# Second-layer sums in PSUM, one scratch pool, first w1 operands made earlier

## The chip, the core and the metric

One core of one Trainium2 chip. The metric is the device time of one execution in microseconds (us), median of several runs. TensorE is PE, VectorE DVE, ScalarE ACT, GpSimd POOL; SP is the queue that issues all transfers.

## What is computed

Linear attention on 4 batches of 8 heads (576 tokens, 64 wide), then two layers on the 2304 tokens of width 512:

```python
# attention, per head; phi(x) = [exp(p), exp(-p)], p = x@w_phi - max|x@w_phi|
kv = k_p^T v;  z = sum(k_p);  x = (q_p kv) / (q_p z + 1e-6)
# first layer, 512 -> 2048 -> 512
h = x @ w_in;  x = max(0.01*h, h) @ w_out
# second layer: 4 experts of 512 -> 1024 -> 512, mixed by normalised domain_probs
for e in range(4): out += p[:, e:e+1] * (max(x @ w1[e], 0) @ w2[e])
```

## The kernel before

All large products are made in three matmuls of float32r operands: a value is split into a high half (`hi`, a copy that rounds) and a low half (`lo`, the difference), and hi*hi, hi*lo and lo*hi are summed in PSUM (`PASS`).

The program is one plan: a list of (time, function) sorted by time (line 816), so the text order of attention steps (`TIMES`, line 39, stretched by `LO` and `HI`) and of first-layer steps (`moe1_group`, line 557) is set by numbers. Attention of batch b+1 runs beside the first layer of batch b. The instructions are then ordered per engine by the tile framework, which may run a later one first when an earlier one still waits. A pool is a ring of equal buffers; a tile waits until one is free.

Attention works pair of heads by pair: loads `kraw` and `qraw`, key features (`kp`, `kt`), `kv`, query features (`pc`, `mb`, `e`, split into `qh` and `ql`), numerators (`nf`), the division by way of DRAM (`ds`, `dr`, `rb`), and the result `xr`, split into `xh` and `xl`. Its scratch tiles of 2304 bytes come from `ap_` (`N_A` = 17 buffers, line 104), opened on the right side of SBUF; the first layer's `hs` and `g` come from `up` (`N_U` = 4, line 98). Line 107 chooses. In the first layer each of 64 blocks F (16 per batch) has an up product (`moe1_up`, tile `hp`), the leaky relu (`hs`, `g`, split into `gt`) and, in groups of four blocks, down products (`moe1_down`, tile `op`), summed into `acc`, one per batch. The last group, after the loops, holds only down products (line 814).

The second layer uses Strassen-like products: tokens in 3 blocks j of two halves of 384, and for each of 16 pairs c of w1 column blocks seven products of half-size operands (`PRODUCTS`, line 652), 48 steps k = 16 j + c. Operands of the tokens (`x2_steps`, line 602: b11, t1, b21, t2, b22, t3, t4, each split) are cut from `acc`; their raw differences lie in `xt`; the halves lie three to a buffer, five buffers to a block, from the list `kind` (`xp` or `x2p`). The difference and the low half are made on POOL, the high half on ACT. Operands of w1: `w2_raw` (line 660) loads two raw blocks into `r`, makes four sums on POOL, and `w2_split` (line 677) makes `wuh` on ACT and `wul` on POOL; w2 is split in `w2_split_d`. All of these pools are opened at line 819, when the first layer's pools are closed, over the same addresses; a tile waits only for the old tiles that it covers.

A step runs `up_a` (products 1, 5, 2, 6, 3, 7), the split of the next step's w1, `down(k-1, 1)`, `up_b` (product 4), `down(k-1, 0)`. In `up_a` product 1 goes to px, is copied to py (the start of product 6's sum), product 2 is added in px; product 5 goes to pv, is copied to ss, product 3 is added in pv. The sums pv + ss and py + ss go to SBUF (`c`), and `relu` makes the high half gh on ACT and the low half gl on VectorE. `down` multiplies gh and gl by w2, and VectorE adds p times the result to `ob`.

Of the kernel before, what the change touches and what calls it, by code (L numbers as in the profile page):

```python
# [16 lines left out]
DF = 128  # L17
# [51 lines left out]
N_U = 4  # L69
N_A = 17  # L70
# [10 lines left out]
def body(ctx, tc, kT, qT, vh, w_phi, w_in, w_out, probs, w1, w2, out):  # L81
# [14 lines left out]
    left, right = ExitStack(), ExitStack()  # L96
    RIGHT = "right"
    up = opened(left, "up", N_U)
    wp = opened(left, "wp", N_W)
    wrp = opened(left, "wrp", 4)  # L100
# [3 lines left out]
    ap_ = opened(right, "ap", N_A, side=RIGHT)  # L104
    vp = opened(right, "vp", 2, side=RIGHT)

    def unit(name, dt=F32):
        pool = up if name in ("hs", "g") else ap_
        return pool.tile([128, S], dt, tag="u", name=name)
# [76 lines left out]
    def k_feat(b, hp, g):  # L186
        if g == 0:
            kfs[b, hp] += (
                xp.tile([128, 2, 4, 2, DF], F32, tag="x", name="kp"),
                ap_.tile([128, 2, 2, DF], F32, tag="u", name="kt"),  # L190
            )
# [24 lines left out]
        nc.vector.tensor_reduce(  # L216
            out=m[0:r, 0:nb], in_=pv, op=ALU.max, axis=AX.X, apply_absolute_value=True
        )
        if INPL[b] or nb == 8:
            y = pv  # L220
        else:
            y = ap_.tile([128, 4, DF], F32, tag="u", name="ky")[0:r, 0:nb]
# [15 lines left out]
    def kv_side(b, hp, h):  # L238
# [18 lines left out]
        if h == 1:  # L257
            if "n" in DIRECT[b]:
                kv = ap_.tile([128, 4, 128], F32, tag="u", name="kv")
# [3 lines left out]
            kvh = ap_.tile([128, 4, 128], F32R, tag="u", name="kvh")  # L263
            kvl = ap_.tile([128, 4, 128], F32R, tag="u", name="kvl")
# [395 lines left out]
    def w2_raw(c):  # L660

        r = m2["r"].tile([128, 8, 256], F32, tag="r", name="r")
        nc.sync.dma_start(out=r[:, 2:4].rearrange("p a f -> p (a f)"), in_=w1[2 * c])
        nc.sync.dma_start(out=r[:, 0:2].rearrange("p a f -> p (a f)"), in_=w1[2 * c + 1])
        r2 = m2["r2"].tile([128, 2, DM], F32, tag="r2", name="r2")
        for t in range(2):
            nc.sync.dma_start(out=r2[:, t], in_=w2[2 * c + t])
        for o, x, y, op in (
            (4, 0, 1, ALU.add),
            (5, 4, 2, ALU.subtract),  # L670
            (6, 2, 0, ALU.subtract),
            (7, 3, 5, ALU.subtract),
        ):
            nc.gpsimd.tensor_tensor(out=r[:, o], in0=r[:, x], in1=r[:, y], op=op)  # L674
        return r, r2
# [143 lines left out]
    for name, bufs in (("r", 1), ("r2", 1), ("wu", 4), ("wd", 2), ("h", 4), ("sum", 2), ("ob", 1)):  # L819
        m2[name] = opened(left, "m2" + name, bufs)  # L820
    for name, bufs in (("px", 2), ("py", 1), ("pv", 1), ("po", 4)):
        m2[name] = opened(left, name, bufs, space=bass.MemoryType.PSUM)
    m2["y"] = m2["py"].tile([128, 512], F32, tag="y", name="py")[:, 0:TH]
    n = NB * NC2
    raw = w2_raw(0)
    w2_split(0, raw)
    w2_split_d(0, raw)
    nxt = []
    for k in range(n):
# [12 lines left out]
        if raw:  # L842
            w2_split_d(k + 1, raw)
# [5 lines left out]
    right.close()  # L849
# [33 lines left out]
```

## Time and profile before

| | |
|---|---|
| Median of 3 runs (lowest, highest) | 1439.45 us (1437.5, 1463.09) |
| Profiled execution: own time, span | 1447.1 us, 1445.3 us |
| PE busy | 1399.8 us, 97% of the span |
| DVE, ACT, POOL busy | 884.1, 657.6, 605.0 us |
| Mean granted clock of PE, whole span | 0.982 |
| Attention alone, then beside the first layer | 0 to about 100, to about 540 us |
| First layer alone | to 677 us |
| Second layer | to the end |

Matmuls are pipelined, so a busy PE need not be at its peak; idle time of another engine costs nothing by itself. In a timeline row the bracket gives the idle time of the engine before it and what ended it. The views are of the profiled execution.

### The profile page before, as it was taken

The page shows a single profiled execution, that of the slowest core. Times are in us where ns is not written, and L with a number is a line of the kernel's source. Part 1 is how long each engine was busy: PE and PEld are TensorE (multiplying, and loading weights), DVE is VectorE, ACT ScalarE, POOL GpSimd, SP SyncE. Part 2 cuts the span into 40 slices and gives each one's busy share as a digit, 9 for nine tenths or more (in the row PEclk, how much of TensorE's full clock was granted, in tenths as well). Part 3 has the DMA queues.
Part 4 walks back from the last instruction along what each step waited for, and adds up shares of the span by engine and source line. Part 5 has one row for each costly group of instructions (what it writes and reads, how often), then busy time and mean ns, then how long its engine had stood idle before and what let it go on. Part 6 is the DMA issues. An engine that isn't in the chain of part 4 may idle for free.

```text
span 1445.3 us, 20868 instructions
## 1 busy us (share of the span) xinstructions
PE 1399.8 (97%) x8105; PEld 1282.1 (89%) x8105; DVE 884.1 (61%) x1270; ACT 657.6 (45%) x1201; POOL 605.0 (42%) x413
## 2 busy tenths in 40 slices
PE   8969998999999989999999999999999999999998
PEld 5758988999899989999789899989989999999997
DVE  4459888757676655653546556555566455655655
ACT  4537665656565733533433433353433333333432
POOL 2222101111111122402966656687665665665651
PEclk9969999999999999999999999999999999999999
DMA  5346474323333222321212221221212123222121
GB/s 191 90 133 220 175 257 132 108 76 114 92 108 94 70 68 66 95 83 47 74 56 75 71 73 59 73 102 60 87 59 73 59 81 110 59 73 73 59 73 44
DMA packets 77266, 134.11 MB, mean 93 GB/s; under 512 B 12016, under 2 KB 21360, under 8 KB 77168
## 3 DMA queue, kind: packets, MB, share of 16 engines
q1 hardware_dynamic: 77168, 132.79, 28.8%
q8 instruction: 63, 1.03, 0.3%
q14 instruction: 35, 0.29, 0.1%
HBM read 119.51 MB, written 13.18 MB: 92 GB/s over the span
## 4 chain that ended last, share of the span: by engine, by line
PE 82%; DMA 7%; DVE 5%; POOL 3%; issue 2%; ACT 1%; SPq 0%; DVEq 0%; POOLq 0%; ACTq 0%
PE po L770 26%; PE op L542 12%; PE hp L510 11%; PE py L699 10%; PE px L699 6%; PE pv L699 6%; PE kvp L250 5%; DMA rb<-dr 3%; PE nm L342 2%; PE pk L211 2%; DMA w<-w 1%; DMA qraw<-qT 1%; POOL wul L683 1%; DMA r<-w 1%; PE pq L296 1%
## 5 line engine op out<-in xcount | busy, mean ns | idle before, releaser
L770 PE MATMUL po<-wd,gh 128*128 128x512 f32 x1152 | 387.9, 392 | 0.2 <-ACT gh L713 0.2
L784 DVE SCALAR_TENSOR_TENSOR ob<-po,pe,ob 128x512 f32<-128x512 f32 x270 | 193.5, 747 | 174.7 <-PE po L770 174.1
L770 PEld LDWEIGHTS po<-wd,gh 128*128 128x128 f32 x1152 | 214.7, 188 | 32.9 <-ACT gh L713 0.5
L683 POOL TENSOR_TENSOR wul<-r,wuh 128x1024 fp32r<-128x1024 f32 x96 | 203.2, 2134 | 93.5 <-ACT wuh L682 93.5
L303 POOL PARTITION_ALL_REDUCE mb<-pc x32 | 72.3, 2261 | 403.6 <-ACT pc L301 319.1
L674 POOL TENSOR_TENSOR r<-r 128x256 f32<-128x256 f32 x192 | 148.0, 792 | 216.5 <-DMA r<-w 213.5
L542 PE MATMUL op<-gt,wt 128*128 128x288 f32 x1536 | 224.8, 300 | 12.0 <-DVE gt L122 9.1
L542 PEld LDWEIGHTS op<-gt,wt 128*128 128x128 f32 x1536 | 211.8, 191 | 16.0 <-DVE gt L122 10.0
L770 PE MATMUL po<-wd,gl 128*128 128x512 f32 x576 | 225.4, 391 | 0.5 <-DVE gl L714 0.5
L510 PE MATMUL hp<-xh,wt 128*128 128x288 f32 x1024 | 217.6, 298 | 4.5 <-ACT xh L121 4.2
L510 PEld LDWEIGHTS hp<-xh,wt 128*128 128x128 f32 x1024 | 168.6, 189 | 6.4 <-ACT xh L121 4.5
L714 DVE SCALAR_TENSOR_TENSOR gl<-s,gh 128x384 fp32r<-128x384 f32 x96 | 137.8, 1437 | 32.4 <-ACT gh L713 32.4
L682 ACT CAST wuh<-r 128x1024 fp32r<-128x1024 f32 x96 | 86.7, 941 | 149.6 <-issue 89.8
L510 PE MATMUL hp<-xl,wt 128*128 128x288 f32 x512 | 152.8, 299 | 0.4 <-DVE xl L122 0.4
L699 PE MATMUL py<-xo,wuh 128*128 128x384 f32 x576 | 149.3, 340 | 0.6 <-ACT s L741 0.6
L770 PEld LDWEIGHTS po<-wd,gl 128*128 128x128 f32 x576 | 108.2, 188 | 18.9 <-DVE gl L714 0.8
L690 POOL TENSOR_TENSOR wd<-r,wd 128x1024 fp32r<-128x1024 f32 x48 | 116.6, 2429 | 6.9 <-ACT wd L689 6.9
L699 PEld LDWEIGHTS py<-xo,wuh 128*128 128x128 f32 x576 | 106.1, 189 | 8.4 <-ACT s L741 1.1
L699 PE MATMUL px<-xo,wuh 128*128 128x384 f32 x384 | 99.6, 340 | 0.2 <-ACT py L735 0.2
L699 PE MATMUL py<-xo,wul 128*128 128x384 f32 x288 | 97.7, 339 | 2.1 <-POOL wul L683 2.1
L699 PE MATMUL pv<-xo,wuh 128*128 128x384 f32 x384 | 99.4, 340 | 0.0
L510 PEld LDWEIGHTS hp<-xl,wt 128*128 128x128 f32 x512 | 96.9, 189 | 1.1 <-DVE xl L122 0.7
(104 smaller groups left out, 2201.1 us busy)
## 6 DMA issues: line engine op xcount, KB each, us to landing
r<-w SPq DMA_DIRECT2D x192, 256.0 KB, 2.6
wr<-w SPq DMA_DIRECT2D x96, 256.0 KB, 2.9
qraw<-qT SPq DMA_DIRECT2D x32, 288.0 KB, 5.1
r<-w_out SPq DMA_DIRECT2D x9, 1024.0 KB
r<-w_in SPq DMA_DIRECT2D x8, 1024.0 KB, 7.6
w<-w SPq DMA_DIRECT2D x32, 256.0 KB, 2.7
v<-vh SPq DMA_DIRECT2D x16, 384.0 KB
kraw<-kT SPq DMA_DIRECT2D x16, 288.0 KB, 9.6
```

The lines of the kernel that those rows point to most:

```text
L250: nc.tensor.matmul(kvp[:, a * 128 : (a + 1) * 128], lhsT=lhs, rhs=v[0:r, c, h * D : h * D + 128], start=(c == 0), stop=(c == 4),)
L303: nc.gpsimd.partition_all_reduce(mb, pc, 128, bass_isa.ReduceOp.absmax)
L510: nc.tensor.matmul(hp[:, n, 0:HS], lhsT=wi[:, a, kk * 128 : (kk + 1) * 128], rhs=x[z][:, kk, n * HS : (n + 1) * HS], start=(kk == 0 and i ...
L542: nc.tensor.matmul(op[:, n, 0:HS], lhsT=wt1[1, C * GF + f][:, a, d * 128 : (d + 1) * 128], rhs=gts[C * GF + f][:, z, n * HS : (n + 1) * HS ...
L674: nc.gpsimd.tensor_tensor(out=r[:, o], in0=r[:, x], in1=r[:, y], op=op)
L682: nc.scalar.copy(out=h, in_=x)
L683: nc.gpsimd.tensor_tensor(out=l, in0=x, in1=h.bitcast(F32), op=ALU.subtract)
L690: nc.gpsimd.tensor_tensor(out=d[:, 1], in0=r2, in1=d[:, 0].bitcast(F32), op=ALU.subtract)
L699: nc.tensor.matmul(out, lhsT=ws[w][:, AOPS[a], kk * 128 : (kk + 1) * 128], rhs=xo[z][:, kk], start=first and n == 0, stop=n == 5, skip_gro ...
L714: nc.vector.scalar_tensor_tensor(out=gl[:, at], in0=src, scalar=0.0, in1=gh[:, at].bitcast(F32), op0=ALU.max, op1=ALU.subtract,)
L770: nc.tensor.matmul(op, lhsT=(gh, gl)[z][:, 2 * f + t, q : q + 128], rhs=d[:, w, f], start=n == 0, stop=n == 5,)
L784: nc.vector.scalar_tensor_tensor(out=o, in0=op, scalar=ps, in1=o, op0=ALU.mult, op1=ALU.add)
```

## The change

- `up` and `ap_` become one pool `up` of 19 buffers; the right side is gone, and `vp` is opened between the first layer's pools.
- `x2p` has 3 buffers instead of 4 and is opened at the start of the second layer, at the lowest address, over the scratch pool. Block 0 takes its first three buffers and its `xt` from `xp`, and two from `x2p`; block 1 one from `x2p` (its first) and four from `xp`. Block 0's differences and low halves are made on VectorE, four of its seven steps in the last first-layer batch and three after its pools are closed.
- `w2_raw` is divided: w1's raw tile becomes two of half the size (`r` loaded, `rs` sums; 4 buffers instead of 1), w2's goes to `w2_raw_d`. For step 0 both w1 functions run in the last first-layer group, with r and rs from `wp` and the halves from `xp`.
- In `up_a` the sums go to PSUM, pv + ss to pv itself and py + ss to a new bank pz; px has one bank instead of two.

```diff
-N_U = 4
-N_A = 17
+N_U = 19
...
     up = opened(left, "up", N_U)
     wp = opened(left, "wp", N_W)
+    vp = opened(left, "vp", 2)
     wrp = opened(left, "wrp", 4)
...
-    ap_ = opened(right, "ap", N_A, side=RIGHT)
-    vp = opened(right, "vp", 2, side=RIGHT)
 
     def unit(name, dt=F32):
-        pool = up if name in ("hs", "g") else ap_
-        return pool.tile([128, S], dt, tag="u", name=name)
+        return up.tile([128, S], dt, tag="u", name=name)
...
-        kind = [xp, xp, xp, xp, 0] if j != 1 else [0, 0, xp, xp, xp]
+        kind = ([xp, xp, xp, 0, 0], [0, xp, xp, xp, xp], [xp, xp, xp, 0, 0])[j]
...
+        eng = nc.vector if j == 0 else nc.gpsimd
+
         def diff(out, f, g, halves):
             for o, n, at in pieces(*halves):
-                nc.gpsimd.tensor_tensor(
+                eng.tensor_tensor(
...
-                    raw.append(x2p[0].tile([128, 3, 2, TH], F32, tag="x", name="xt"))
+                    raw.append((x2p[0] if j else xp).tile([128, 3, 2, TH], F32, tag="x", name="xt"))
...
                 nc.scalar.copy(out=hi[:, :, o : o + n], in_=r)
-                nc.gpsimd.tensor_tensor(
+                eng.tensor_tensor(
...
-        r = m2["r"].tile([128, 8, 256], F32, tag="r", name="r")
+        pool, tag = (m2["r"], "r") if m2 else (wp, "w")
+        r, s = (pool.tile([128, 4, 256], F32, tag=tag, name=n) for n in ("r", "rs"))
...
-        r = raw[0]
-        hi = m2["wu"].tile([128, 7, 256], F32R, tag="wu", name="wuh")
-        lo = m2["wu"].tile([128, 7, 256], F32R, tag="wu", name="wul")
-        for h, l, x in ((hi[:, 0:4], lo[:, 0:4], r[:, 1:5]), (hi[:, 4:7], lo[:, 4:7], r[:, 5:8])):
+        r, s = raw
+        if m2:
+            hi, lo = (m2["wu"].tile([128, 7, 256], F32R, tag="wu", name=n) for n in ("wuh", "wul"))
+        else:
+            hi, lo = (xp.tile([128, 7, 256], F32R, tag="x", name=n) for n in ("wuh", "wul"))
+        for h, l, x in ((hi[:, 0:3], lo[:, 0:3], r[:, 1:4]), (hi[:, 3:7], lo[:, 3:7], s)):
...
+        Z = m2["pz"].tile([128, 512], F32, tag="z", name="pz")[:, 0:TH]
         Y = m2["y"]
-        ss, c = sums(), sums()
+        ss = m2["sum"].tile([128, 2, TH], F32, tag="s", name="s")
...
-        nc.vector.tensor_tensor(out=c[:, 0], in0=V, in1=ss[:, 1], op=ALU.add)
+        nc.vector.tensor_tensor(out=V, in0=V, in1=ss[:, 1], op=ALU.add)
         product(k, 7, Y, False)
-        nc.vector.tensor_tensor(out=c[:, 1], in0=Y, in1=ss[:, 0], op=ALU.add)
-        relu(g, 1, c[:, 0])
-        relu(g, 3, c[:, 1])
+        nc.vector.tensor_tensor(out=Z, in0=Y, in1=ss[:, 0], op=ALU.add)
+        relu(g, 1, V)
+        relu(g, 3, Z)
...
-            a = [(b, attn_end)] + spread(x2_steps(0), b + 0.1, b + 0.9)
+            early = x2_steps(0)
+            a = spread(early[:4], b + 0.1, b + 0.9)
         plan += m + a
     plan += spread(moe1_group(B * NF // GF), B, B + 0.1)
+    plan += [(B + 0.005, lambda: w2_split(0, w2_raw(0)))]
...
     left.close()
-    for name, bufs in (("r", 1), ("r2", 1), ("wu", 4), ("wd", 2), ("h", 4), ("sum", 2), ("ob", 1)):
+    x2p.append(opened(left, "x2p", 3))
+    for name, bufs in (("r", 4), ("r2", 1), ("wu", 4), ("wd", 2), ("h", 4), ("sum", 2), ("ob", 1)):
         m2[name] = opened(left, "m2" + name, bufs)
-    for name, bufs in (("px", 2), ("py", 1), ("pv", 1), ("po", 4)):
+    for name, bufs in (("px", 1), ("py", 1), ("pv", 1), ("pz", 1), ("po", 4)):
...
+    for f in early[4:]:
+        f()
     n = NB * NC2
-    raw = w2_raw(0)
-    w2_split(0, raw)
-    w2_split_d(0, raw)
+    w2_split_d(0, w2_raw_d(0))
```

## Rows read from the trace of the kernel before

**Rows 1.** The page, parts 1 (busy us, share of the span) and 4 (last chain).

```profile
PE 1399.8 (97%) x8105; PEld 1282.1 (89%) x8105; DVE 884.1 (61%) x1270; ACT 657.6 (45%) x1201; POOL 605.0 (42%) x413
...
PE po L770 26%; PE op L542 12%; PE hp L510 11%; PE py L699 10%; PE px L699 6%; PE pv L699 6%; PE kvp L250 5%; DMA rb<-dr 3%; PE nm L342 2%; PE pk L211 2%; DMA w<-w 1%; DMA qraw<-qT 1%; POOL wul L683 1%; DMA r<-w 1%; PE pq L296 1%
```

**Rows 2.** Stretches: us, busy of each engine (x instructions), granted clock, DMA share, GB/s.

```profile
0.00:110.00 110.00, 89.50 (x379) 67.92 (x380) 50.58 (x84) 48.13 (x103) 24.97 (x15) 0.86 0.46 142
110.00:200.00 90.00, 88.11 (x579) 79.30 (x579) 80.01 (x135) 59.52 (x123) 11.94 (x5) 1.00 0.64 223
200.00:540.00 340.00, 327.57 (x2386) 316.37 (x2386) 239.18 (x380) 199.97 (x395) 45.49 (x23) 0.99 0.33 99
540.00:677.00 137.00, 137.00 (x1021) 136.90 (x1020) 77.17 (x97) 54.08 (x90) 31.85 (x20) 0.99 0.23 70
677.00:690.00 13.00, 10.48 (x49) 9.59 (x48) 3.80 (x5) 7.55 (x11) 10.52 (x7) 0.87 0.36 122
690.00:720.00 30.00, 28.12 (x134) 23.70 (x132) 17.64 (x22) 12.78 (x21) 30.00 (x20) 1.00 0.17 53
720.00:760.00 40.00, 38.14 (x184) 34.62 (x185) 17.86 (x27) 14.72 (x25) 25.63 (x21) 0.96 0.22 69
```

**Rows 3.** Timeline of ACT: copies of px, steps 0, 5 and 46 (start, us, ...).

```profile
682.45 0.46 ACT L735 COPY py<-px 128x384 f32<-128x384 f32 x1 [0.90 <-PE px L699]
...
766.13 0.47 ACT L735 COPY py<-px 128x384 f32<-128x384 f32 x1
...
1410.29 0.46 ACT L735 COPY py<-px 128x384 f32<-128x384 f32 x1 [1.43 <-DVE gl L714]
```

**Rows 4.** Timeline of SP's queue, first 30 us.

```profile
9.28 1.87 SPq L172 DMA_DIRECT2D qraw<-qT  x3
...
29.20 0.52 SPq L172 DMA_DIRECT2D qraw<-qT  x1
```

**Rows 5.** Timeline, end of the first layer and start of the second.

```profile
664.26 12.87 PE L542 MATMUL op<-gt,wt 128*128 128x288 f32 x96
...
667.49 0.33 SPq L663 DMA_DIRECT2D r<-w  x1
...
670.89 2.94 POOL L674 TENSOR_TENSOR r<-r 128x256 f32<-128x256 f32 x4 [61.18 <-DMA r<-w]
...
678.31 0.45 PE L731 MATMUL py<-xo,wuh 128*128 128x384 f32 x1 [1.18 <-ACT wuh L682]
...
680.76 0.69 PE L699 MATMUL px<-xo,wul 128*128 128x384 f32 x1 [1.29 <-POOL wul L683]
```

**Rows 6.** Groups by line and form: busy us, mean ns of one, idle before.

```profile
L714 DVE SCALAR_TENSOR_TENSOR gl<-s,gh 128x384 fp32r<-128x384 f32 x96 | 137.8, 1437 | 32.4 <-ACT gh L713 32.4
...
L683 POOL TENSOR_TENSOR wul<-r,wuh 128x1024 fp32r<-128x1024 f32 x48 | 115.5, 2407 | 90.7 <-ACT wuh L682 90.7
...
L683 POOL TENSOR_TENSOR wul<-r,wuh 128x768 fp32r<-128x768 f32 x48 | 89.4, 1862 | 2.8 <-ACT wuh L682 2.8
...
L682 ACT CAST wuh<-r 128x1024 fp32r<-128x1024 f32 x48 | 50.5, 1052 | 137.0 <-issue 89.8 <-PE py L699 20.8 <-POOL r L674 13.1
...
L555 DVE TENSOR_TENSOR acc<-op,acc 128x576 f32<-128x576 f32 x48 | 36.2, 755 | 33.0 <-PE op L542 32.8
```

**Rows 7.** Timeline of PE, 690 to 765 us: its two longest waits.

```profile
721.05 0.45 PE L699 MATMUL py<-xo,wul 128*128 128x384 f32 x1 [2.09 <-POOL wul L683]
...
741.06 0.44 PE L699 MATMUL px<-xo,wul 128*128 128x384 f32 x1 [0.80 <-POOL wul L683]
```

**Rows 8.** Tile view of gh: durations ns min/median/max, first and last start.

```profile
L714 DVE SCALAR_TENSOR_TENSOR gl<-s,gh x96: 548/1068/2820, 688.6 to 1433.4; 128x384 fp32r<-128x384 f32 x96
...
L714 DVE SCALAR_TENSOR_TENSOR gl<-px,gh x48: 557/559/560, 685.5 to 1427.9; 128x384 fp32r<-128x384 f32 x48
```

**Rows 9.** Timeline, 351 to 365 us: hs of F = 25, and ql of head 6.

```profile
351.25 0.65 ACT L522 ACTIVATE hs<-hp 128x576 f32<-128x576 f32 x1 [0.19 <-PE hp L510]
...
365.27 0.19 PEld L342 LDWEIGHTS nm<-ql,kvh 128*128 128x128 f32 x1
```

More of the change, by code (lines that the diff above doesn't have):

```diff
@@ L93, in opened @@
         )
-    left, right = ExitStack(), ExitStack()
-    RIGHT = "right"
+    left = ExitStack()
     up = opened(left, "up", N_U)
     wp = opened(left, "wp", N_W)
+    vp = opened(left, "vp", 2)
     wrp = opened(left, "wrp", 4)
@@ L189, in k_feat @@
                 xp.tile([128, 2, 4, 2, DF], F32, tag="x", name="kp"),
-                ap_.tile([128, 2, 2, DF], F32, tag="u", name="kt"),
+                up.tile([128, 2, 2, DF], F32, tag="u", name="kt"),
             )
@@ L221, in k_feat @@
         else:
-            y = ap_.tile([128, 4, DF], F32, tag="u", name="ky")[0:r, 0:nb]
+            y = up.tile([128, 4, DF], F32, tag="u", name="ky")[0:r, 0:nb]
         nc.vector.tensor_tensor(
@@ L258, in kv_side @@
             if "n" in DIRECT[b]:
-                kv = ap_.tile([128, 4, 128], F32, tag="u", name="kv")
+                kv = up.tile([128, 4, 128], F32, tag="u", name="kv")
                 nc.scalar.copy(out=kv, in_=kvp.rearrange("p (a f) -> p a f", f=128))
@@ L262, in kv_side @@
                 return
-            kvh = ap_.tile([128, 4, 128], F32R, tag="u", name="kvh")
-            kvl = ap_.tile([128, 4, 128], F32R, tag="u", name="kvl")
+            kvh = up.tile([128, 4, 128], F32R, tag="u", name="kvh")
+            kvl = up.tile([128, 4, 128], F32R, tag="u", name="kvl")
             kv3 = kvp.rearrange("p (a f) -> p a f", f=128)
@@ L660, in w2_raw, with w2_raw_d @@
     def w2_raw(c):
-        r = m2["r"].tile([128, 8, 256], F32, tag="r", name="r")
+        pool, tag = (m2["r"], "r") if m2 else (wp, "w")
+        r, s = (pool.tile([128, 4, 256], F32, tag=tag, name=n) for n in ("r", "rs"))
         nc.sync.dma_start(out=r[:, 2:4].rearrange("p a f -> p (a f)"), in_=w1[2 * c])
         nc.sync.dma_start(out=r[:, 0:2].rearrange("p a f -> p (a f)"), in_=w1[2 * c + 1])
+        for o, x, y, op in (
+            (s[:, 0], r[:, 0], r[:, 1], ALU.add),
+            (s[:, 1], s[:, 0], r[:, 2], ALU.subtract),
+            (s[:, 2], r[:, 2], r[:, 0], ALU.subtract),
+            (s[:, 3], r[:, 3], s[:, 1], ALU.subtract),
+        ):
+            nc.gpsimd.tensor_tensor(out=o, in0=x, in1=y, op=op)
+        return r, s
+    def w2_raw_d(c):
         r2 = m2["r2"].tile([128, 2, DM], F32, tag="r2", name="r2")
@@ L667, in w2_raw @@
             nc.sync.dma_start(out=r2[:, t], in_=w2[2 * c + t])
[L668 to L675, printed above, removed]
-    def w2_split(k, raw):
-        r = raw[0]
-        hi = m2["wu"].tile([128, 7, 256], F32R, tag="wu", name="wuh")
-        lo = m2["wu"].tile([128, 7, 256], F32R, tag="wu", name="wul")
-        for h, l, x in ((hi[:, 0:4], lo[:, 0:4], r[:, 1:5]), (hi[:, 4:7], lo[:, 4:7], r[:, 5:8])):
+        return r2
+    def w2_split(k, raw):
+        r, s = raw
[4 more added lines that the diff above has]
+        for h, l, x in ((hi[:, 0:3], lo[:, 0:3], r[:, 1:4]), (hi[:, 3:7], lo[:, 3:7], s)):
             nc.scalar.copy(out=h, in_=x)
@@ L684, in w2_split, with w2_split_d @@
         wo[k] = (hi, lo)
-    def w2_split_d(k, raw):
-        r2 = raw[1]
+    def w2_split_d(k, r2):
         d = m2["wd"].tile([128, 2, 2, DM], F32R, tag="wd", name="wd")
@@ L717, in relu @@
         )
-    def sums():
-        return m2["sum"].tile([128, 2, TH], F32, tag="s", name="s")
     def up_a(k):
@@ L798, in first2 @@
         w1_split(0, 0)
-    def attn_end():
-        right.close()
-        x2p.append(opened(right, "x2p", 4, side=RIGHT))
     plan = attn(0, -P0, 0) + [(-P0 * (1 - FI0), first), (-P0 * (1 - FI1), first2)]
@@ L832, in body @@
             nxt = x2_steps(j + 1)
-        raw = w2_raw((k + 1) % NC2) if k + 1 < n else None
+        last = k + 1 == n
+        if not last:
+            raw, raw_d = w2_raw((k + 1) % NC2), w2_raw_d((k + 1) % NC2)
         up_a(k)
-        if raw:
+        if not last:
             w2_split(k + 1, raw)
@@ L841, in body @@
             down(k - 1, 0)
-        if raw:
-            w2_split_d(k + 1, raw)
+        if not last:
+            w2_split_d(k + 1, raw_d)
         if c >= 2 and c % 2 == 0 and nxt:
@@ L848, in body @@
     left.close()
-    right.close()
 def kernel(q, k, v, w_phi, moe_w_in, moe_w_out, moe2_domain_probs, moe2_w1, moe2_w2):
```

## The prediction

> **What bounds the kernel now.** I read the page's busy table and slices first. TensorE (PE) is busy 97% of the span and the other engines 61% or less [rows 1], so time can only be won where PE idles or where its clock is low. The view by stretches shows where that is [rows 2]: up to 110 us PE is busy 89.50 of 110 at a mean granted clock of 0.86; from 110 to 540 it idles about 14 us; 540 to 677 is full. Between 677 and 760, where the second layer starts, it is busy 10.48 of 13, 28.12 of 30 and 38.14 of 40 us, with a granted clock of 0.87 in the first of these and 0.96 in the last. From there on the layer keeps PE's own pace: one step (42 matmuls of 384 columns, 36 of 512) takes 644.16 us / 41 = 15.71 us, from the px copies of steps 5 and 46 [rows 3], whatever VectorE does beside it. So the second layer is PE's pace plus a bad start.
>
> The first layer and the attention are PE-bound too from 110 us on, but with a thin cover: attention tiles wait for buffers. The 17 buffers of `ap_` are handed out in program order. Sorting the plan's entries by their times, tiles 1 to 17 of that pool hold kraw of pairs 0 to 2 and qraw of heads 0 to 5, and just these nine loads go out by 11 us; the next tiles are not loads, and the seventh qraw goes out at 29.20 us, when a buffer has come free [rows 4]. This in-order rule decides what the merged pool does.
>
> **The change part by part.**
>
> *First w1 operands in the last first-layer group.* Before, the raw w1 tile is loaded at 667.49 and combined by POOL by 673.83, but the split waits for the last first-layer matmul (664.26 + 12.87 = 677.13), because its buffers lie over the first layer's weights. PE then idles 1.18 us, starts on the high halves and idles 1.29 us for the low ones [rows 5]. The granted clock of 0.87 over these 13 us [rows 2] is at most 13 x 0.13 = 1.7 us more; part of it falls on idle time, so I take 1.3. In all 1.18 + 1.29 + 1.3 = 3.8 us. After, r and rs come from `wp`, whose up-weights come free as the last ups end, and the two splits from `xp`, where the last x operands are free when the downs begin at 664.26. Load 3.4 us (667.49 to 670.89, before 664 here), four POOL combinations 2.94, then two copies of at most 1.05 and POOL subtractions of 1.86 and 2.41 [rows 5, 6] end near 671, six before they are due. POOL stands idle there (61 us before 670.89 [rows 5]). On SP the two loads pass nothing that PE waits for: the last group has no weight left to load. Were that cover gone, the old 3.8 us would return. The PSUM banks are the remaining wait: if the last `op` lies where px and py come, its eviction (0.76 us) costs 0.8. I take -3.8, bounds -4.1 and -3.0. The w2 load keeps its place (it waits for the same weights), and is wanted a step later, behind down(0).
>
> *POOL after the start.* POOL is busy 30.00 of 30 us from 690 to 720 [rows 2]: splits of block 0, raw sums, and all seven operand steps of token block 1. PE waits on its low halves 2.09 us at 721.05 and 0.80 at 741.06 [rows 7], and the 0.96 clock over 40 us is 1.6 us. Check: the px copies of steps 0 and 5 stand 83.68 us apart [rows 3] against 5 x 15.71 = 78.55, so 5.1 us are lost. After, the first splits (1.86 + 2.41) and the sums (2.94) are done, raw tiles are four half-size buffers instead of one, so the next load no longer waits for the previous split, and block 1's t-steps come later (next part). I take -5.0, bounds -5.3 (the check and the shorter step) and -3.
>
> *x operands.* Block 0's subtractions move from POOL to VectorE. Four steps run in the first layer's last batch, where VectorE is busy 77 of 137 us [rows 2]; b22, t3 and t4 come at its end, on `x2p`, now laid over the scratch pool and free when the last of its tiles is read, as the w1 load shows that waited for the same place until 667.49 [rows 5]. Three subtractions of 768 elements are left then. VectorE needs 0.755 us for 576 [rows 6], so about 1.0 each (estimate), with three copies of under 1.05: done by 674, wanted after 24 to 36 matmuls of step 0, at 15.71 / 78 = 0.2 us each 5 to 7 us after 677. Cost nothing; the cover is 8 us.
> `x2p` shrinks from 4 to 3 buffers. In program order it holds two of block 0 (b22/t3 and t4), one of block 1 (b11/t1), then block 1's raw tile. That fourth tile gets a buffer only when block 0's t3 is read for the last time, at product 7 of step 15. So t1 to t4 of block 1, four differences and four low halves of about 1.86 us, 14.9 us of POOL, fall into step 16, beside POOL's regular 2.9 + 4.3 + 2.4 = 9.6 us per step: 24.5 against 15.7. PE can meanwhile do product 4 of step 15, products 1 and 2 and the downs that are open, 72 matmuls or 14.5 us. Lower bound 0 (all covered), upper 24.5 - 15.7 = 8.8; the same steps ran in the POOL-bound start, where PE waited 2.09 and 0.80 us for POOL [rows 7], so I take +2.
>
> *Sums in PSUM.* c goes to V in place and to a new bank pz, px has one bank. VectorE's gl from SBUF takes 1437 ns on average, from PSUM 559 [rows 6, 8]: 96 x 0.88 = 84 us of VectorE time. It is idle 39% of the span [rows 1] and the steps keep PE's pace: gain 0. The new wait: px, V are freed by gl, then wanted by the next step's products 1 and 5. px is read two products before the step's end and pz not by PE; the chain product, copy, add, relu, gl is some 4 us of 15.7. Cost 0, bound +1.
>
> *One scratch pool.* 17 + 4 buffers become 19, in one order. While only attention runs (to 101 us) it has 19 instead of 17. PE idles 20.5 us there [rows 2]. I handed 19 buffers out in order over the first write and last read of all 536 tiles of the two pools in the trace: the load at 29.20 could go out at 16.5, the later ones of that batch 1 to 6 us earlier. Bounds: nothing, and -8 (2/19 of some 80 us in which attention is alone). Later the pool couples the layers: hs of F = 25 is written at 351.25 out of its own four buffers [rows 9]. In the merged order, tiles ahead of it that are not yet released at that time number 34 by the trace; with 19 buffers, 16 must go first, and the sixteenth is ql of head 6, read at 365.27 [rows 9]. So at the old pace the first layer would stop for up to 14 us around F = 20 to 26, less elsewhere (5 or under), none in the first batch. PE has three hp/op buffers, six gt and the attention's own matmuls against this; attention also gets ahead by 1 to 3 us from the two extra buffers. Bounds 0 and +14; near the middle of what is not covered, +3. The first 110 us I put at -3. Sum 0, bounds -8 and +14.
>
> The sum: -3.8 - 5.0 + 2 + 0 = -6.8 us. The profiled execution took 1447.1 us (span 1445.3), so 1440.3; it lies 7.65 us above the median of 1439.45, and the same difference gives **1432.5 us** on that scale.
>
> **A rule against the change.** gl with both inputs in SBUF ranges from 548 to 2820 ns, with one in PSUM from 557 to 560 [rows 8]; POOL works beside both. So two SBUF inputs is what VectorE pays for when POOL runs, and block 0's moved subtractions have two. The Trainium skill, "SBUF — State Buffer", section "Who interferes with whom", says that a VectorE instruction with two SBUF inputs and a GpSimd instruction reading SBUF exclude each other, whoever starts first holding the shared port pair for its whole length. The rows on gl agree.
>
> **Rivals.**
> 1. *The scratch pool holds back the first layer* (the other sign). Place: hs of F = 20 to 26, 300 to 370 us; price up to 14 us less the cover; it decides the sign if more than 9.8 us of the wait reach PE. Then 1432.5 + 11 = 1443.5, slower than before. For: loads wait for buffers [rows 4], so attention cannot simply run faster. Against: PE idles only 12.4 of 340 us between 200 and 540 [rows 2], so there is other work at hand. Chance 0.25.
> 2. *Step 16 stalls*: 24.5 against 15.7 of POOL is all seen by PE: 8.8 instead of 2 gives 1439.3, no gain. For: the same operations made PE wait on `wul` at 721 [rows 7]. Against: product order and downs give cover. 0.10.
> 3. *More buffers speed the first batch*, -8 instead of -3 and no later hold (0 instead of +3): 1432.5 - 8 = 1424.5. For: the chain that ended last runs through rb<-dr and qraw transfers [rows 1]. Against: from 110 to 200 VectorE is busy 80 of 90 [rows 2]. 0.12.
> 4. *VectorE and POOL collide*: b22, t3, t4 each take 2.82 us [rows 8] and push POOL's first splits. Starting at 667.5, 3 x 2.82 + 3 x 1.05 = 11.6 us ends at 679.1, still before the 682 at which b22 is wanted; only if the three wait until 677.13 does t4 end at 688.7, some 4 us late: 1436.5. This is the rule of the Trainium skill above, "SBUF — State Buffer", as it would act here. 0.03.
>
> **How the numbers follow.** The forecast (start repaired, pool neutral, 1427 to 1437) has 0.50. Low end: bounds -4.1 - 5.3 + 0 - 8 = -17.4, so 1422. High end: -3 - 3 + 4 + 8 = +6, so 1445.5 (the pool's wait with 6 us of cover). Outside lie the full 14 us and the full stall together, about 0.15. A difference under 2%, 29 us, is about what a measurement of this kernel cannot tell from no change; every case above lies inside it. Beyond on the fast side is only a first batch far shorter, 0.03; on the slow side a hold of the first layer in every batch, 0.02; within, 0.95.
>
> **What would show it.** Step 0's px copy near 678.5 (minus the shift of the first layer) instead of 682.45, a granted clock of 1.00 from 677 to 760, no wait of PE on `wul` before step 16; POOL no longer full in 690 to 720; gl at about 0.56 us; a cluster of `xt` on POOL only at step 15 or 16 and PE waiting there for `xo`. If the first-layer end moves from 677.1 by more than 5 us, the pool is the reason: later with hs waiting for nothing the profile shows (rival 1), earlier with the first-layer matmuls starting earlier (rival 3). The forecast is wrong if PE shows new idle time between 200 and 540 us of over 9 us beyond today's 12, or if step 16 is longer than 24 us.

## The result and the profile after

The changed kernel takes 1450.45 us (median of 4; 1450.15 to 1451.19), the kernel before 1440.9 beside it: ratio 1.0074, interval 1.0056 to 1.0092. The ratio is of mean times and leaves out one slow run of the kernel before, of 1463.09 us, without which that kernel's median is 1439.45 us. The changed kernel is slower by 0.7%, less than the 2% that the chances go by, but clearly not 1432.5, and outside the range of 1422 to 1445.5. The profiled execution took 1451.19 us (span 1449.4) against 1447.1 (1445.3).

The page of the changed kernel, part 1 (busy us, share of the span, instructions), answers to [rows 1]:

```profile
PE 1400.6 (97%) x8105; PEld 1271.7 (88%) x8105; DVE 808.0 (56%) x1285; ACT 664.4 (46%) x1201; POOL 570.8 (39%) x398
```

VectorE lost 76 us of work in all (84 were foretold for gl alone, and block 0's operands came to VectorE) and GpSimd 34; PE's own work did not become shorter. The stretches of the changed kernel (columns as in [rows 2]; cut where its own first layer ends, with one more around step 16):

```profile
0.00:110.00 110.00, 89.21 (x411) 68.63 (x411) 52.67 (x89) 50.33 (x107) 23.28 (x15) 0.88 0.43 134
...
200.00:540.00 340.00, 336.71 (x2481) 327.11 (x2480) 247.56 (x384) 202.78 (x397) 36.14 (x16) 0.99 0.33 99
...
661.00:674.00 13.00, 11.27 (x59) 9.88 (x58) 3.93 (x7) 7.35 (x12) 8.18 (x8) 1.00 0.49 163
674.00:704.00 30.00, 29.17 (x146) 25.83 (x145) 13.74 (x22) 11.48 (x18) 28.01 (x24) 1.00 0.28 88
704.00:744.00 40.00, 39.75 (x196) 35.20 (x195) 17.49 (x29) 15.34 (x25) 22.46 (x17) 1.00 0.21 66
905.00:966.00 61.00, 52.54 (x235) 44.53 (x234) 22.21 (x37) 27.05 (x44) 59.89 (x42) 0.92 0.23 78
```

Between 200 and 540 us PE's idle time fell from 12.4 us to 3.3, and the start of the second layer is repaired: granted clock 1.00 in all three stretches. New is the last line: 8.5 us of idle PE, GpSimd full, clock 0.92 (another 61 x 0.08 = 4.9 us, an estimate). The kernel before has PE busy 60.43 of 61 us in the corresponding stretch, 923 to 984 us, at a clock of 1.00.

The timelines give the rest of the loss. Copies of px on ACT in the changed kernel, steps 5, 16, 17 and 46, as in [rows 3]:

```profile
744.79 0.46 ACT L736 COPY py<-px 128x384 f32<-128x384 f32 x1 [1.69 <-DVE gl L717]
...
920.10 0.46 ACT L736 COPY py<-px 128x384 f32<-128x384 f32 x1 [0.23 <-DVE gl L717]
949.54 0.46 ACT L736 COPY py<-px 128x384 f32<-128x384 f32 x1 [0.62 <-DVE gl L717]
...
1414.23 0.46 ACT L736 COPY py<-px 128x384 f32<-128x384 f32 x1 [1.69 <-DVE gl L717]
```

From the px copy of step 16 to that of step 17 it takes 29.44 us, and the quiet steps (between the copies of 8 and 15, and of 24 and 46) have gone from 15.67 to 16.03 us. Below, as in the expectations, the time of step k runs from the px copy of step k - 1 to its own, so this is the time of step 17. With the same marks (the first write of attention results `xr`, the last first-layer matmul, px copies of steps 0, 7, 15, 24, 47, the last matmul) both profiled executions split so:

| stretch, us | before | after | difference |
|---|---|---|---|
| to the first xr | 54.0 | 49.4 | -4.6 |
| to the last first-layer matmul | 623.1 | 611.9 | -11.2 |
| to px of step 0 | 5.3 | 1.3 | -4.0 |
| steps 0 to 7 | 116.0 | 114.3 | -1.7 |
| steps 7 to 15 | 125.4 | 128.3 | +2.9 |
| steps 15 to 24 | 141.7 | 156.7 | +15.0 |
| steps 24 to 47 | 358.0 | 365.8 | +7.8 |
| rest | 17.8 | 17.9 | +0.1 |

The first line varies between executions: 48.5 to 52.0 us in the experiments below whose scratch pool is the changed kernel's, 52.7 to 54.0 in the kernel before and those made from it. In e3, the changed kernel with two scratch pools, it is 49.0, so the pool does not make the 4.6 us; part of them may be scatter, and the cause is open. The other lines sum to +8.9 us, against 10.7 by the ratio.

### The profile page after: what moved, and what is told of

Read it like the earlier page. It is cut to its first block, busy times and chain, and to the rows that moved or that the text cites. A ratio compares the mean times of both kernels' runs of the same rounds, so it can differ in the third digit from the quotient of the medians.

```text
span 1449.4 us, 21159 instructions
## 1 busy us (share of the span) xinstructions
PE 1400.6 (97%) x8105; PEld 1271.7 (88%) x8105; DVE 808.0 (56%) x1285; ACT 664.4 (46%) x1201; POOL 570.8 (39%) x398
## 4 chain that ended last, share of the span: by engine, by line
PE 81%; ACT 6%; DMA 4%; POOL 3%; DVE 3%; issue 2%; SPq 0%; ACTq 0%; DVEq 0%; POOLq 0%
PE po L771 25%; PE op L538 14%; PE hp L506 13%; PE py L702 7%; PE pv L702 6%; PE kvp L246 6%; PE px L702 4%; ACT wd L692 3%; PE nm L338 3%; PE pk L207 2%; DVE gl L717 2%; ACT gh L716 1%; DMA rb<-dr 1%; POOL xo L642 1%; DMA qraw<-qT 1%
## 5 line engine op out<-in xcount | busy, mean ns | idle before, releaser
L771 PE MATMUL po<-wd,gh 128*128 128x512 f32 x1152 | 382.2, 393 | 2.2 <-ACT gh L716 2.2
L785 DVE SCALAR_TENSOR_TENSOR ob<-po,pe,ob 128x512 f32<-128x512 f32 x270 | 186.8, 745 | 271.0 <-PE po L771 270.7
L299 POOL PARTITION_ALL_REDUCE mb<-pc x32 | 79.1, 2474 | 386.9 <-ACT pc L297 324.2
L538 PE MATMUL op<-gt,wt 128*128 128x288 f32 x1536 | 221.7, 298 | 4.7 <-DVE g L520 4.0
L687 POOL TENSOR_TENSOR wul<-r,wuh 128x768 fp32r<-128x768 f32 x48 | 88.9, 1853 | 215.5 <-ACT wuh L686 215.5
L670 POOL TENSOR_TENSOR rs<-r 128x256 f32<-128x256 f32 x96 | 69.1, 741 | 224.8 <-DMA r<-w 224.8
L687 POOL TENSOR_TENSOR wul<-rs,wuh 128x1024 fp32r<-128x1024 f32 x48 | 115.0, 2396 | 0.0
L702 PE MATMUL px<-xo,wuh 128*128 128x384 f32 x384 | 103.3, 349 | 6.7 <-DVE gl L717 1.5
L692 ACT CAST wd<-r 128x1024 fp32r<-128x1024 f32 x48 | 50.6, 1054 | 102.1 <-PE po L771 98.8
```

The source lines that it names most:

```text
L299: nc.gpsimd.partition_all_reduce(mb, pc, 128, bass_isa.ReduceOp.absmax)
L538: nc.tensor.matmul(op[:, n, 0:HS], lhsT=wt1[1, C * GF + f][:, a, d * 128 : (d + 1) * 128], rhs=gts[C * GF + f][:, z, n * HS : (n + 1) * HS ...
L670: nc.gpsimd.tensor_tensor(out=o, in0=x, in1=y, op=op)
L692: nc.scalar.copy(out=d[:, 0], in_=r2)
L702: nc.tensor.matmul(out, lhsT=ws[w][:, AOPS[a], kk * 128 : (kk + 1) * 128], rhs=xo[z][:, kk], start=first and n == 0, stop=n == 5, skip_gro ...
L771: nc.tensor.matmul(op, lhsT=(gh, gl)[z][:, 2 * f + t, q : q + 128], rhs=d[:, w, f], start=n == 0, stop=n == 5,)
```

## The experiments

Ratios are of mean times, to the kernel before on the same chip, with 95% intervals; its medians were 1443.12 us beside e1 to e4, 1442.05 beside e5 to e8, 1445.86 beside e9 and e10, 1442.37 beside e11 and e12.

### Why the step is longer

The changed kernel in step 10 (timeline; product 6 into py, then product 1 of the next step into px):

```profile
828.64 0.51 PE L702 MATMUL py<-xo,wuh 128*128 128x384 f32 x2
828.84 0.49 ACT L716 ACTIVATE gh<-px 128x384 fp32r<-128x384 f32 x1
...
829.37 0.56 DVE L717 SCALAR_TENSOR_TENSOR gl<-px,gh 128x384 fp32r<-128x384 f32 x1 [0.41 <-ACT gh L716]
829.52 0.33 PE L702 MATMUL py<-xo,wul 128*128 128x384 f32 x1
...
829.98 0.62 PE L702 MATMUL px<-xo,wuh 128*128 128x384 f32 x2
```

Product 1 starts 457 ns after the matmul ahead of it, where 175 to 182 is usual: px is read by gl until 829.93. A second place of 283 ns follows within px. Together 0.28 + 0.11 us: the step's whole 0.36 to 0.39. My first theory was the single px bank.

**e1: px two banks, po three.**

```diff
-("px", 1), ("py", 1), ("pv", 1), ("pz", 1), ("po", 4)
+("px", 2), ("py", 1), ("pv", 1), ("pz", 1), ("po", 3)
```

> The changed kernel with two px banks again, paid for by one po bank (px 2, po 3 instead of 1 and 4); the sums stay in PSUM. Changed kernel: steps of 16.03 us, two gaps at each product 1 on px (457 ns where 178 is usual, and one of 283 in place of 176). Theory, the single px bank: product 1 of the next step waits until VectorE has read px for gl; with two banks a step is 15.7 us again, 47 x 0.36 = 17 us less, about 1433.5. Rival, the sums in PSUM (or the divided w1 tiles) cost the time by themselves: steps stay at 16.03 and the time at 1450.

1467.6 us, ratio 1.0150 (1.0107 to 1.0194); step 16.55. No gap before px is left, but another order came with the banks: product 7 stands right behind product 6 and waits for the copy of py. The waits of PE in this kernel from 660 to 1430 us (total us, times, longest):

```profile
PE py L702 <- ACT s L742: 23.2, 40, 1.1
```

So the wait went, another came, and the time is neither the theory's nor the rival's; nothing follows on the bank alone, since po lost one too.

**e2: the kernel before with px one bank.**

```diff
-("px", 2), ("py", 1), ("pv", 1), ("po", 4)
+("px", 1), ("py", 1), ("pv", 1), ("po", 4)
```

> The kernel before with one px bank instead of two, nothing else; sums stay in SBUF. Theory, the single px bank costs the step: steps grow from 15.67 to about 16.0 us, 47 x 0.36 = 17 us more, about 1457. Rival, the sums in PSUM cost it: steps stay at 15.67 us and the time at 1440.

1443.41 us, ratio 1.0004 (0.9973 to 1.0035), step 15.63. One bank for px costs nothing by itself; the first theory fell.

**e5: the changed kernel with both sums in SBUF, px one bank.**

```diff
-Z = m2["pz"].tile(...)
+ss, c = two tiles of m2["sum"]
-tensor_tensor(out=V, in0=V, in1=ss[:, 1]);      relu(g, 1, V)
+tensor_tensor(out=c[:, 0], in0=V, in1=ss[:, 1]); relu(g, 1, c[:, 0])
-tensor_tensor(out=Z, in0=Y, in1=ss[:, 0]);      relu(g, 3, Z)
+tensor_tensor(out=c[:, 1], in0=Y, in1=ss[:, 0]); relu(g, 3, c[:, 1])
```

> The changed kernel with the two sums of a step written to an SBUF tile again and the pz bank gone; px keeps one bank, all else stays. Theory (the sums in PSUM, and the order of matmuls that comes with them, make the longer step): the 457 ns start-to-start between a py and a px matmul goes, the step falls from 16.03 to about 15.65 us, 47 steps give -18 us, 1432 us against the changed kernel's 1450; steps 16 and 17 still hold about 44 us together. Rival (the divided w1 tiles with their four buffers make it): the step stays at 16.03 us and the time at 1450.

1441.26 us, ratio 0.9980 (0.9942 to 1.0017), step 15.62. The same place of step 9 in its timeline:

```profile
810.21 0.49 ACT L716 ACTIVATE gh<-px 128x384 fp32r<-128x384 f32 x1 [2.29 <-PE px L702]
...
810.74 0.56 DVE L717 SCALAR_TENSOR_TENSOR gl<-px,gh 128x384 fp32r<-128x384 f32 x1 [0.62 <-ACT gh L716]
...
810.89 0.34 PE L702 MATMUL py<-xo,wul 128*128 128x384 f32 x1
811.07 0.40 PE L770 MATMUL po<-wd,gh 128*128 128x512 f32 x1
...
812.22 0.39 PE L770 MATMUL po<-wd,gh 128*128 128x512 f32 x1
812.44 0.51 PE L702 MATMUL px<-xo,wuh 128*128 128x384 f32 x2
```

Six down matmuls stand between product 6 and the next product 1 and cover gl, which ends at 811.30. The gain against the changed kernel is 9 us by the medians and 12.7 by the profiled executions, not 18: the quiet steps give 3.3 and 8.6 us, but steps 15 to 24 still take 156.6, since another thing holds them (below), and this execution's first xr came 2.6 us later.

**e6: the kernel before with the sums in PSUM** (the reverse edit, and px one bank).

```diff
-ss, c = sums(), sums()
+ss = sums(); Z = m2["pz"].tile(...)   # V in place, Z = Y + ss[:, 0]
-("px", 2), ("py", 1), ("pv", 1), ("po", 4)
+("px", 1), ("py", 1), ("pv", 1), ("pz", 1), ("po", 4)
```

> The kernel before with the sums in PSUM alone: V added to in place, a pz bank for the other, px one bank. Theory (sums in PSUM): step 16.03 us instead of 15.67, 47 steps give +17 us, about 1458 us, ratio 1.012. Rival (divided w1 tiles): step 15.65, 1441 us, ratio 1.000.

1455.16 us, ratio 1.0082 (1.0048 to 1.0115), step 16.00; the 458 ns from py to px stands in each step. With e2 as its partner this is the sums alone: +12.5 us from step 7 to 47 by the two profiles (125.1 to 128.0, 141.4 to 142.9, 357.3 to 365.4).

**e11: only V's sum in PSUM** (the other sum in SBUF, no pz bank).

```diff
-tensor_tensor(out=Z, in0=Y, in1=ss[:, 0]);       relu(g, 3, Z)
+tensor_tensor(out=c[:, 1], in0=Y, in1=ss[:, 0]); relu(g, 3, c[:, 1])
```

> The changed kernel with only the sum of products 3 and 6 in PSUM (added to V in place); the other sum goes to an SBUF tile, and the pz bank is gone. Theory (the add into V in place is what orders product 1 of the next step right behind product 6): the step stays at 16.0 us, the 457 ns from a py to a px matmul stands once per step, about 1450 us. Rival (the pz bank and its sum do it): step 15.62, about 1441 us.

Step 16.03 and 458 ns, as the theory has it. The time, 1462.81 us (ratio 1.0124, 1.0070 to 1.0178), is 12 more than expected: steps 15 to 24 take 166.2 us here. Why, is told in the last section. That the other sum is free shows in e12 below (step 15.62 with it in pz). So the add in place, V = V + ss, makes the longer step. In every kernel run with it and one px bank, product 1 stands right behind product 6 in the quiet steps; in e2, e5, e8 to e10 and e12, which have one px bank and not this add, down matmuls stand between. Why the framework's ordering of the instructions turns on this add was not tested. One candidate: the sum in place keeps the pv bank in use until gl has read it (until 832.08 in step 10 above), while e5 is done with the bank after the add (at 812.34 in step 9). A run with two pv banks would test it.

### What holds steps 16 to 19

PE's waits in the changed kernel from 905 to 960 us (timeline, idle time in brackets):

```profile
925.16 0.61 PE L702 MATMUL px<-xo,wuh 128*128 128x384 f32 x2 [0.82 <-DVE gl L717]
929.55 0.69 PE L702 MATMUL pv<-xo,wuh 128*128 128x384 f32 x1 [3.06 <-POOL xo L642]
934.37 1.21 PE L702 MATMUL py<-xo,wuh 128*128 128x384 f32 x2 [1.06 <-ACT s L742]
948.97 0.97 PE L771 MATMUL po<-wd,gh 128*128 128x512 f32 x3 [2.01 <-ACT gh L716]
956.55 0.44 PE L702 MATMUL px<-xo,wul 128*128 128x384 f32 x1 [1.26 <-POOL wul L687]
```

and GpSimd's x operand work, its first rows and its last (17 rows of xt and xo in all, 35.4 us of the 48.2 from 912.60 to 960.79):

```profile
912.60 3.66 POOL L619 TENSOR_TENSOR xt<-acc 128x768 f32<-128x768 f32 x2
916.22 1.85 POOL L619 TENSOR_TENSOR xt<-acc,xt 128x768 f32<-128x768 f32 x1
918.04 1.85 POOL L642 TENSOR_TENSOR xo<-xt,xo 128x768 fp32r<-128x768 f32 x1
...
958.78 2.01 POOL L619 TENSOR_TENSOR xt<-acc,xt 128x384 f32<-128x384 f32 x2
```

**e4: four x2p buffers** (and two w1 tiles instead of four, for room).

```diff
-x2p.append(opened(left, "x2p", 3)); ("r", 4)
+x2p.append(opened(left, "x2p", 4)); ("r", 2)
-[0, xp, xp, xp, xp]
+[xp, xp, xp, xp, xp]
```

> The changed kernel with four buffers in x2p instead of three, paid for by two r buffers instead of four. Changed kernel: steps 16 and 17 take 14.97 + 29.44 us, 12.3 over two usual steps. Theory, block 1's raw tile waits for an x2p buffer until step 15 and the steps of blocks 1 and 2 then fill POOL: with the fourth buffer steps 16 and 17 are usual ones, -12 us, about 1438. Rival 1, POOL's total load stalls PE wherever these steps are put: the stall moves to steps 1 to 4 with about the same size, 1450. Rival 2, four r buffers are needed at the start: steps 1 to 5 lose up to 5 us, 1443.

1453.31 us, ratio 1.0064 (1.0041 to 1.0086). Steps 15 to 24 fall to 143.4 us, no more than nine steps of the longer pace take, with both blocks' operands still on GpSimd. But the second block's work now runs at the start, as rival 1 has it: steps 0 to 7 take 123.1 instead of 114.3, and the last op of the first layer waits 4.0 us for `acc`. How much of that is due to the two r buffers that are gone (rival 2) was not separated. The longest wait in those steps:

```profile
695.07 0.69 PE L702 MATMUL pv<-xo,wul 128*128 128x384 f32 x1 [4.85 <-POOL wul L687]
```

**e9: e5 with all x operands on VectorE, tiles as in the changed kernel.**

```diff
-eng = nc.vector if j == 0 else nc.gpsimd
+eng = nc.vector
```

> The kernel of e5 (sums in SBUF) with the x operands of all blocks on VectorE, and their tiles as in the changed kernel (three buffers for the second layer, so that the second block waits for the first block's tiles). Theory (GpSimd's own load in that stretch, 28 of 30 us busy, is what holds steps 16 and 17): the two steps together fall from 45.9 us to about 34, and the time to 1441 - 11 = 1430 us. Rival (the tiles come free late, and the operands are late on any engine): the two steps stay at 44 us or more, and the time at 1441.

1439.56 us, ratio 0.9937 (0.9901 to 0.9973). Steps 15 to 24 take 156.4 us as in e5 (156.6), but otherwise divided: steps 16 and 17 fell from 45.8 to 39.8 us, between the theory's 34 and the rival's 44, and steps 18 and 19 grew from 32.7 to 38.6. GpSimd is now busy 36.29 of the 61 us and PE still only 48.89; it waits for VectorE. The stretch (columns as in [rows 2]):

```profile
905.00:966.00 61.00, 48.89 (x228) 41.84 (x227) 44.79 (x58) 25.89 (x43) 36.29 (x22) 0.94 0.23 78
```

and its longest wait in the timeline:

```profile
951.13 1.01 PE L702 MATMUL px<-xo,wuh 128*128 128x384 f32 x2 [5.61 <-DVE gl L717]
```

The operands are late on either engine, so GpSimd's load alone does not explain the stall. That it has no part is not shown: what VectorE saved in steps 16 and 17 it lost in 18 and 19, where it now makes the third block's operands (e8 and e10 below show that price), and no run has the second block alone on VectorE with late tiles. That late tiles matter on both engines is shown, by e4 on GpSimd and by e8, which differs from e9 in the tiles alone, on VectorE (148.3 against 156.4 us).

**e8 and e10: tiles that need no wait.** Both are e5 with the second block's operands in five tiles of the x pool and on VectorE; the third block's are on VectorE in e8, on GpSimd in e10.

```diff
-kind = (..., [0, xp, xp, xp, xp], ...)[j];  eng = nc.vector if j == 0 else nc.gpsimd
+kind = (..., [xp, xp, xp, xp, xp], ...)[j]; eng = nc.vector                            # e8
+kind = (..., [xp, xp, xp, xp, xp], ...)[j]; eng = nc.vector if j < 2 else nc.gpsimd    # e10
```

> The changed kernel with the sums in SBUF, the x operands of all three blocks on VectorE, and those of the second block in five tiles of the x pool, so that their steps need not wait for the first block's tiles. Theory (GpSimd's load with two blocks of x operands is what holds steps 16 and 17): no step over 19 us, steps 16 and 17 together about 31 us, start steps as in the changed kernel, about 1420 us, ratio to the kernel before 0.985. Rival (the x operands stall the matmuls on whichever engine they are made, as VectorE's own reads of PSUM wait behind them): some 8 to 12 us come back in the first steps or in steps 16 and 17, about 1430 us.

> The kernel of e8 with the third block's x operands on GpSimd again; the second block's stay on VectorE. Theory (in e8 the one wait of 4.6 us left in steps 16 to 20 is px behind VectorE's gl, which stands behind the third block's x operands there): that wait goes, steps 16 to 19 together fall from 70.3 us to about 65, and the time from 1436 to about 1431 us, ratio to before 0.990. Rival (GpSimd stalls the matmuls with them as in e5, by its w1 operands): a wait of POOL of 3 us or more in steps 16 to 20, time 1436 to 1441 us.

e8: 1436.18 us, ratio 0.9934 (0.9896 to 0.9971), 16 more than the theory had. Steps 15 to 24 take 148.3 us: both sides had a part, since steps 18 and 19 still lose 6 us, with a wait of 4.6 us of px for gl on VectorE; and steps 0 to 7 take 117.3 (112.9 in e5). e10: 1429.39 us, ratio 0.9881 (0.9814 to 0.9948); steps 16 to 19 take 63.6 us (70.3 in e8, about 65 foretold), steps 15 to 24 141.6, PE full in the stretch (columns as before):

```profile
905.00:966.00 61.00, 60.75 (x302) 54.28 (x301) 33.03 (x48) 29.17 (x49) 53.73 (x38) 1.00 0.26 87
```

GpSimd does 53.73 of 61 us here and harms nothing. What is left is at the start, where VectorE now makes the second block's operands; PE's timeline there:

```profile
691.50 1.01 PE L702 MATMUL px<-xo,wuh 128*128 128x384 f32 x2 [5.38 <-DVE gl L717]
```

Steps 0 to 7 take 120.7 us (112.9 in e5). The intervals of e8 and e10 overlap, and e8's profiled execution, the fastest of its ten, took 1429.11 us, no longer than e10's 1429.7: the steps show what the third block's place is worth there, the times do not show which kernel is faster.

**e12: e10 with the other sum in the pz bank.**

> The kernel of e10 with the other sum (products 7 and 5) in the pz bank, as in the changed kernel; only V's sum is in SBUF. Theory (only the sum in V in place costs the step anything): step 15.62 us and about 1429 us as e10, with VectorE's gl for that sum near 0.56 us. Rival (any sum in PSUM costs the step): step 16.0 us, about 1445 us.

1428.77 us, ratio 0.9895 (0.9863 to 0.9928), step 15.62: as e10, and faster than both given kernels. So not any sum in PSUM costs the step, only the one in place. e12 keeps of the change all but that sum and the second block's tiles and engine.

### What made the first layer shorter

**e3: the changed kernel with two scratch pools again** (4 and 17).

```diff
-up = opened(left, "up", 19)
+up = opened(left, "up", 4); ap_ = opened(left, "ap", 17)
```

> The changed kernel with the scratch divided again, 4 buffers for hs and g and 17 for attention, in place of 19 for all. Changed kernel: the first layer ends at 661.3 us, 15.8 earlier than before. Theory, the merged pool gives the 15.8 us: the end moves back to about 677 us and the time to 1466. Rival, the token operands made on VectorE give it, since POOL is then free for attention's reductions: the end stays near 661 us and the time near 1450.

1460.3 us, ratio 1.0111 (1.0074 to 1.0147). The first layer ends at 669.7 us, between theory and rival. From the first xr to the last first-layer matmul it takes 620.7 us, against 611.9 in the changed kernel and 623.1 before: the common pool gives 8.8 of the 11.2 us. How, is seen in marks of the two (first xr at 49.0 in e3 and 49.4 in the changed kernel): hs of F = 20 is written later with one pool, at 301.5 against 295.3, and hs of F = 25 (as in [rows 9]) by 11 us, but the third batch's first xr comes at 315.5 against 320.9, and hs of F = 44 at 522.5 against 529.8. The rows of F = 25, in the changed kernel and in e3:

```profile
357.26 0.65 ACT L518 ACTIVATE hs<-hp 128x576 f32<-128x576 f32 x1
...
346.31 0.65 ACT L520 ACTIVATE hs<-hp 128x576 f32<-128x576 f32 x1 [0.17 <-PE hp L508]
```

**e7: the first block's x operands on GpSimd.**

```diff
-eng = nc.vector if j == 0 else nc.gpsimd
+eng = nc.gpsimd
```

> The changed kernel with the first block's x operands back on GpSimd (VectorE in the changed kernel). Theory (with GpSimd free of them the first layer's last stretch ends earlier: the 7 us of the first layer's gain that the scratch pool does not explain): the first layer ends at about 668 us instead of 661, the whole takes about 1457. Rival (that gain is of another part, the move to VectorE is worth nothing in the first layer): end at 661 and about 1450 us.

1454.49 us, ratio 1.0071 (1.0037 to 1.0104); the first layer ends at 660.3 us, and the same stretch takes 611.1. The move to VectorE is worth nothing in the first layer. The remaining 2.4 us are no more than scatter may be: the stretch takes 608.0 to 613.0 us in the other kernels with the common pool, but for e4, whose last op waits. The median is 4 us above the changed kernel's; the profiled execution, at 1450.33 the fastest of the ten, shows no place for them.

## Why the prediction was wrong, point by point

**First w1 operands early: right.** -3.8 us foretold, -4.0 measured. The end of the first layer and the start of the second, as in [rows 5], without a gap:

```profile
654.76 6.54 PE L538 MATMUL op<-gt,wt 128*128 128x288 f32 x48
661.13 0.34 PE L732 MATMUL py<-xo,wuh 128*128 128x384 f32 x1
```

**GpSimd after the start: right.** -5.0 foretold. Steps 0 to 7 fell by 1.7 us; seven steps of the longer pace, 7 x 0.36 = 2.5, are in that, so -4.2, within the bounds; e5, which has not the longer pace, took 112.9 us against 116.0, or -3.1. Part of this gain is only moved: where e4 puts the second block's operands back at the start, steps 0 to 7 take 123.1 us.

**Sums in PSUM: the step that failed most plainly.** I put them at 0 with a bound of +1, as "px is read two products before the step's end". That held for the order of the kernel before, which I took over unasked; with V added in place, product 1 moved to where its bank is still being read. Cost: +2.9 and +7.8 us in the quiet steps and, by the count above, 2.5 in the first seven; 12.5 from step 7 to 47 with nothing else changed (e6 against e2). What I had added up was right: gl takes 0.56 us (changed kernel's tile view of gh, as in [rows 8]):

```profile
L717 DVE SCALAR_TENSOR_TENSOR gl<-pv,gh x48: 548/558/559, 670.2 to 1434.5; 128x384 fp32r<-128x384 f32 x48
L717 DVE SCALAR_TENSOR_TENSOR gl<-pz,gh x48: 557/558/559, 670.9 to 1437.4; 128x384 fp32r<-128x384 f32 x48
```

and it was worth nothing, as I had said: with one of these gl from the pz bank (e12) or both from SBUF (e10) the step is the same.

**Three x2p buffers: place and mechanism right, size wrong.** +2 foretold, at most 8.8; +15.0 measured in steps 15 to 24, and 14.9 in e5 without the longer pace (the 29.44 us after the px copy of step 16 are longer than the 24 named as the sign). The place and the reason, a tile that comes free late, are confirmed by e4 and by e8 against e9. The mis-sized term is the work that falls there: I counted 14.9 us of x operands, the trace has 35.4 us between 912.60 and 960.79, as the next block's follow without a pause. And I priced it as a load on GpSimd with cover, while lateness counts on either engine (e9); GpSimd's own share in the stall is not separated.

**One scratch pool: wrong sign of the later part.** I took -3 for the first 110 us and +3 later. The pool gave 8.8 us (e3), just beyond my bound of -8, and not in the first 110 us, where PE's busy time stayed (89.21 against 89.50) and the first xr is as early with two pools (49.0 in e3), but between 200 and 540, where its idle time fell to 3.3 us (8.5 in e3). So rival 3 was right in amount and wrong in place. Rival 1, to which I gave 0.25, had its place and nearly its delay (6.2 us at F = 20 and 11 at F = 25 against e3, up to 14 foretold) and not its price: PE was not idle meanwhile, attention came ahead, and I take it that this lead shortened the first layer later. The order of buffers told who waits; it did not tell that the time was used.

**Rival 2** came, at 15.0 instead of 8.8 us; **rival 4** did not: the last x subtractions on VectorE, at 653.19, took 1.82 us for two, and the start lost nothing to them.

**The range.** Its high end of 1445.5 did not use my own bounds: it took the x2p part at +4 (bound 8.8), the sums at 0 (bound +1) and the pool at +8 (bound +14). With the bounds, -3 - 3 + 8.8 + 1 + 14 = +17.8 us, it would have been about 1457.

In sum: -4.0 - 4.2 - 11.2 on the good side, 2.5 + 2.9 + 15.0 + 7.8 on the other, +8.9 with the rest, where I had -6.8. Two gains were as worked out and a third came unlooked for; two parts priced near nothing took them back.

## What to carry to other kernels

When a result is kept in place in its accumulation bank, ask for the order of the instructions anew: the cost lies not in the read but in what is now queued ahead of the bank's release, and one wait per step times 48 steps outweighs a whole repaired start. When a pool loses a buffer, follow the allocation that now has to wait to the last read it waits for, and count all the work queued behind it, not only the first item. And give a group of tiles room before moving its work to another engine: the move alone only shifted the loss (e9). Then look where the work lands: at the start it cost some 8 to 9 us (e4, e10).

## What the runs showed of the hardware

In e11 one gl with both inputs in SBUF took 11.72 us, usually 0.56 (timeline of VectorE in that kernel, and below it that of GpSimd):

```profile
957.50 0.56 DVE L717 SCALAR_TENSOR_TENSOR gl<-pv,gh 128x384 fp32r<-128x384 f32 x1 [0.56 <-ACT gh L716]
...
959.12 11.72 DVE L717 SCALAR_TENSOR_TENSOR gl<-s,gh 128x384 fp32r<-128x384 f32 x1 [0.59 <-ACT gh L716]
```

```profile
957.60 2.42 POOL L687 TENSOR_TENSOR wul<-rs,wuh 128x1024 fp32r<-128x1024 f32 x1
959.96 2.00 POOL L619 TENSOR_TENSOR xt<-acc,xt 128x384 f32<-128x384 f32 x2
...
969.70 0.73 POOL L670 TENSOR_TENSOR rs<-rs,r 128x256 f32<-128x256 f32 x1
970.98 1.41 POOL L670 TENSOR_TENSOR rs<-r 128x256 f32<-128x256 f32 x2 [0.56 <-DMA r<-w]
```

It ended at 970.84, inside the first pause that GpSimd made after it began (970.43 to 970.98); nine GpSimd instructions, with the one under way, ran meanwhile. The gl from pv at 957.50, beside the same run of GpSimd, took 0.56. PE waited 6.62 us for that gl, and 2.58 for another that took 6.02: most of e11's unexpected loss. The Trainium skill, "SBUF — State Buffer", section "Who interferes with whom", says that VectorE with two SBUF inputs and a GpSimd instruction that reads SBUF shut each other out for the length of one instruction. In e11 nine of GpSimd's instructions went by. Yet in e5 a gl with two SBUF inputs, beside GpSimd without a pause as well, got in after the one instruction under way (its row, then GpSimd's):

```profile
933.66 1.63 DVE L717 SCALAR_TENSOR_TENSOR gl<-s,gh 128x384 fp32r<-128x384 f32 x1 [0.59 <-ACT gh L716]
...
932.51 2.36 POOL L693 TENSOR_TENSOR wd<-r,wd 128x1024 fp32r<-128x1024 f32 x1
934.84 1.73 POOL L670 TENSOR_TENSOR rs<-r 128x256 f32<-128x256 f32 x2
```

So an unbroken run of GpSimd does not always keep such a gl out, and what made the difference no run shows. A sum in the pz bank was not exposed to it: in the changed kernel gl from pz took 0.56 us in the same stretch.
